# Constant matmuls into score banks, mask rows in another order, and a moved step table in an attention-to-experts kernel

## The chip, the cores and the metric

The kernel runs on one core of a Trainium2 chip. The metric is the device time of one execution in microseconds (us), as the median of several runs. A profile is one more execution, recorded by the hardware; its clock for an instruction's start counts from the first instruction. The engines are named as the profile names them: PE is TensorE (matmuls and transposes), PEld its weight loads, DVE is VectorE, ACT is ScalarE, POOL is GpSimd, SP is the engine that issues most DMAs.

## The reference

Clustered attention, then a routed layer of eight experts, then a dense layer.

```python
q_assign = np.argmax(np.einsum('bhsd,hcd->bhsc', q_n, c_n), axis=-1)   # 16 clusters
k_assign = np.argmax(np.einsum('bhsd,hcd->bhsc', k_n, c_n), axis=-1)
mask = q_assign[:, :, :, None] == k_assign[:, :, None, :]
scores = np.where(mask, scale * np.matmul(q, k.transpose(0, 1, 3, 2)), -1e9)
attn = softmax(scores); out = np.matmul(attn, v)       # B=2, H=8, S=768, D=64
...
e_idx = np.argmax(x @ w_gate, axis=1)                  # one of 8 experts for each of 1536 tokens
h = np.maximum(x[mask] @ w1[e], 0.0); ye = h @ w2[e]   # 512 -> 1024 -> 512
out[mask] = gate_w[mask, None] * eom[mask, e, None] * ye
...
h = x @ w_in; g = h * sigmoid(h); out = g @ w_out      # 512 -> 2048 -> 512
```

## The kernel before

**Attention** goes over eight pairs of heads (four in each of two batches), twelve steps a pair, 96 steps in all. A step is 128 queries of one head against all 768 keys. The scores of a step are four matmuls into a two-bank tile `sp` of which two copies exist (`qk_mm`, L398 and L400). The first two multiply `QA` by `KA`, which hold the split values; the second two multiply `QB` by `KB`, whose rows 64 to 79 hold a one-hot cluster number, so that a product of unequal clusters is pushed out of the softmax. DVE takes the minimum of the (negated) scores (`m`, L419), ACT the exponential (`p`, L421), which also frees `sp`. The weights of attention are then split in a high and a low 16-bit part and turned, in one of two ways. In the steps for which `onpe` holds (two of each six, and all of the last twelve), PE transposes them (`ptp`, L445), ACT writes the high part (`pt`, L451) and DVE subtracts to get the low one (`low2`, L456). In the others the high part is a copy by ACT (L430), or by DVE where `dve` says so (L464), POOL subtracts (L465), and a DMA transposes. `pv` then multiplies with the values (L489 to L491) into `o`, and DVE normalises `o` into `xb` (L496 to L498).

Between the steps stand the preparations of the next pair, at steps that a table of numbers gives (`plan`, `prepare`): loads, splits, transposes of q and k (`tp`, L190), products with the centroids (`cl`, L207), the search for the nearest one in four pieces (`best`, L217 to L225, which ends in the one-hot rows `oh`), and the mask rows (`masks`: transposes L365, one ACT operation to `mk`, four DMAs into `QB` and `KB`). The first pair has no step before it: `first` makes its heads, and `masks1` writes their mask rows straight from PSUM, three one-hot tiles at a time. `T` tiles (three PSUM banks) serve all transposes, centroid products, masks and logits.

**Order.** All attention instructions of an engine run in the order in which the code records them: `run` adds a dependency from each to the one before it on its engine. An engine waits at its next instruction, and what is behind waits too.

**The router.** When both heads of a pair are done, `Moe.pair` transposes their output (`xtp`, L717), multiplies by the router's weights (`lg`, L729) and adds to the logits (L736); after a batch's last pair `route` picks experts, ranks the tokens by matmuls (`rk`, L777 to L781) and scatters the rows to the experts' lists by indirect DMAs on POOL (L818). These are generators; `run` calls them so many times a step as a table of small numbers says. Step 84 starts the last pair; its queries are taken in two groups, four tiles then two, so that the last routing covers only two tiles.

**PE fillers.** `warm` issues matmuls of constant ones ahead of the first transposes, and 33 constant matmuls (L1075) stand between the last routing and the first expert. After that the experts (L1000, L1016) and the dense layer (L1246, L1225) run, fed by weights that SP loads and ACT, DVE and POOL split.

Of the kernel before, what the change touches and what calls it, by code (L numbers as in the profile page):

```python
# [30 lines left out]
class Att:  # L31
# [251 lines left out]
    def plan(s, pairs, g0, vg):  # L283

        nc = s.nc
        u = []
        add = lambda r, f: u.append((r, f))
        nx = lambda g: lambda: next(g, None)
        s.v1 = s.load_v(1)
        for r in (-0.5, 0.0, 0.0, 1, 1.5, 2, 3.0, 3.5):  # L290
            add(r, nx(g0))
        for r in (1.5, 1.5, 2.5, 3.5, 4.5, 5.5, 6, 6.5):
            add(r, nx(vg))
        for r in (13.5, 17.5, 23.0, 32.5, 33.5, 40.5, 41.5, 42.5, 44.0):
            add(r, nx(s.v1))
        for r in (-0.5, -0.5, 0.0, 0.5):
            add(r, lambda: s.bgdma.pop(0)())
        for p, (b, hp) in enumerate(pairs):
            o = 12 * p
            for h, r in enumerate((7.0, 10.0) if p == 0 else (1.5, 1.5)):  # L300
                add(o + r, lambda b=b, h=2 * hp + h: s.split_v(b, h))
            if p:
                s.prepare(add, p, pairs[p], o - 12)
        u.sort(key=lambda x: x[0])
        return u

    def prepare(s, add, p, pair, o):

        nc = s.nc
        b, hp = pair  # L310
        z = p == 1
        if not z:
            add(2.5 if p == 2 else o - 12 + -3.0, lambda: s.load_qk(b, hp))
        for i, r in enumerate((-1.0, -1.0) if z else (6.0, 9.5) if p == 2 else [o - 12 + r for r in (6.0, 6.0)]):
            add(r, lambda i=i: s.halves(pair, i))
        hd = [None, None]
        mem = {}
        ch = [None, None]

        def tr(j, a, half):  # L320
            if a == 0 and half == 0:
                hd[j] = s.heads(2 * hp + j, j)
            s.turned(hd[j][1 + 2 * a], s.nqk[pair][a], j, half, (-0.125, 1.0)[a])
            if half:
                src, dst, e = ((hd[j][1][0:64], hd[j][2][0:64], nc.sync), (hd[j][3][64:128], hd[j][4][0:64], nc.sync))[a]
# [11 lines left out]
        for x, r in zip(tr8, (1.5, 1.5, 2.0, 2.5, 3.0, 4.5, 5.5, 5.5) if z else (-1.5, -1.0, -1.0, -0.5, 0.5, 1.5, 3.5, 3.5)):  # L337
            add(o + r, lambda x=x: tr(*x))
        for (j, a), r in zip(((0, 0), (0, 1), (1, 0), (1, 1)), (4.0, 5.0, 6.0, 6.5) if z else (0.5, 1.0, 4.0, 4.0)):
            add(o + r, lambda j=j, a=a: sc(j, a))  # L340
        for i, r in enumerate((5.5, 6.0, 7.0, 7.0, 7.5, 8.5, 9.0, 9.0) if z else (2.5, 2.5, 3.5, 4.5, 5.0, 5.0, 6.0, 7.5)):
            add(o + r, lambda j=i // 4: next(ch[j]))

        def m():
            s.masks(mem['oh'], hd)
            for j in range(2):
                s.ready[b, hp, j] = hd[j]
        add(o + (9.5 if z else 8.0), m)
# [22 lines left out]
    def masks1(s, oh, hd, j):  # L371

        nc = s.nc
        tps = []
        for half in range(2):
            for a in range(2):
                mp = s.T('mp1')
                tps.append(mp)
                for i in range(3):
                    nc.tensor.matmul(mp[64:80, i * 128:(i + 1) * 128], lhsT=oh[:, half * 3 + i, j, a], rhs=s.identb, start=True, stop=True)  # L380
            for a, w in ((0, 2), (1, 4)):
                dst = hd[w][64:80, half * 3:half * 3 + 3]
                src = tps[2 * half + a][64:80, :384].rearrange('p (t n) -> p t n', t=3)
                if a == 0:
                    nc.scalar.activation(dst, src, AF.Copy, scale=-1.0, bias=1.0)
                else:
                    nc.vector.tensor_scalar(dst, src, BIG, None, op0=ALU.mult)
            yield

    def qk_mm(s, st):  # L390
        nc = s.nc
        h, QA, QB, KA, KB = st['hd']
        t = st['t']
        sp = s.ps_s.tile([128, 2, 512], F32, tag='S', name='sp')
        KAf = KA.rearrange('p t n -> p (t n)')
# [12 lines left out]

    def dve(s, st):

        return st['i'] % 12 in (2, 8, 10)

    def soft(s, st):
        nc = s.nc
# [88 lines left out]
    def run(s):  # L503
# [4 lines left out]
        nc = s.nc  # L508
# [15 lines left out]
        st = s.setup()  # L524
        s.consts()
        s.warm(12)
        next(st)
        next(g0)
        next(st)
        next(g0)  # L530
        s.late = []
        s.steps = steps = []
        s.cur = None
# [8 lines left out]
        n = len(steps)  # L542
        done = 0
        i = -1
        todo = []
        while done < n:
            s.now = i
            if i + 1 < n:
                st = steps[i + 1]
# [12 lines left out]
            late = 2 <= i < n + 2 and s.onpe(steps[i - 2])  # L562
            if late and (i - 1 >= n or s.onpe(steps[i - 1])):
                s.low2(steps[i - 2])
                late = False
            if 1 <= i < n + 1:
                (s.turn if s.onpe(steps[i - 1]) else s.low)(steps[i - 1])
            if late:
                s.low2(steps[i - 2])
                late = False  # L570
            while todo and todo[0][0] <= i:
                todo.pop(0)[1]()
            for k in range(3 if i >= n - 12 else 2):
# [12 lines left out]
            if i == 86:  # L586
# [1 line left out]
                    s.bgdma.pop(0)()  # L588
                rg.append(s.route0)
                free = True  # L590
            for k in range((1, 0, 1, 2, 2, 1, 0, 1, 1, 2, 1, 0)[i % 12] if i < n - 12 else (2, 1, 0, 1, 1, 1, 2, 1, 2, 1, 1, 2)[i % 12] if i < n - 2 else (3, 1, 1, 0, 4)[i - n + 2]):
                if rg and (free or not (1 <= i < n - 12 and s.onpe(steps[i - 1]))):
                    x = next(rg[0], 0)
                    free = x == 'free'
                    if x == 0:
                        rg.pop(0)
# [34 lines left out]
class Moe:  # L631
# [112 lines left out]
    def route(s, b, att, g):  # L744
        nc = s.nc
        n = len(g)
# [566 lines left out]
```

## Time and profile before

| | |
|---|---|
| median of 3 runs | 793.61 us (791.09 to 793.64) |
| profiled execution | 794.19 us, of which the span of instructions is 792.5 us |
| PE busy | 742.1 us of the span (94%), 5498 matmuls |
| DVE, ACT, POOL busy | 467.7, 433.7 and 318.1 us |
| mean granted PE clock | 0.97 of full speed |
| first scores, last scores | 15.01 us, 252.37 us |
| first expert's transposes | 278.38 us |

The profiled execution lies 0.6 us over the median. Busy times are sums over the whole span, and stages have different limits; the clock column of a stretch, in which 1.00 is 2.4 GHz and 0.50 is 1.2 GHz, says whether a busy PE is busy at full speed.

### The profile page before, as it was taken

What the parts mean: (1) busy time and instruction counts of PE and PEld (TensorE: products, weight loads), DVE (VectorE), ACT (ScalarE), POOL (GpSimd) and SP (SyncE); (2) the same over time, 40 slices, a digit from 0 to 9 for tenths busy, and PEclk for the clock granted to TensorE, in tenths of its full rate; (3) what the DMA queues carried; (4) which work ended last, traced back from release to release, by engine and by line L of the source; (5) the groups of instructions that cost most, each with busy time, mean ns of one, the idle gap of its engine ahead of it and who ended that gap; (6) DMA issues with size and microseconds to landing.
All of it is one profiled execution on the core that took longest, in us unless ns stands there. A gap on an engine that the chain in (4) does not pass through costs nothing.

```text
span 792.5 us, 14080 instructions
## 1 busy us (share of the span) xinstructions
PE 742.1 (94%) x5498; PEld 625.6 (79%) x5498; DVE 467.7 (59%) x830; ACT 433.7 (55%) x703; POOL 318.1 (40%) x259
## 2 busy tenths in 40 slices
PE   7889999999997799999999999799999999999996
PEld 6788998999887478888978877587687888878885
DVE  6769887977785565555557683789524222232222
ACT  5769889988764435654556663788423222122222
POOL 5677878788631365443334552445300000000000
PEclk8779999999988899999999999999999999999999
DMA  8879998998993377876658735756101000010001
GB/s 270 173 151 215 200 181 176 188 195 179 196 171 121 137 259 229 296 268 230 205 159 285 261 116 191 242 166 207 34 1 53 1 1 0 1 54 0 1 1 55
DMA packets 132983, 116.30 MB, mean 147 GB/s; under 512 B 97607, under 2 KB 103751, under 8 KB 132912
## 3 DMA queue, kind: packets, MB, share of 16 engines
q1 hardware_dynamic: 129632, 109.03, 52.0%
q0 software_dynamic: 3280, 6.33, 2.1%
q8 instruction: 44, 0.72, 0.4%
q14 instruction: 27, 0.22, 0.1%
HBM read 71.67 MB, written 18.45 MB: 114 GB/s over the span
## 4 chain that ended last, share of the span: by engine, by line
PE 53%; DVE 14%; issue 11%; DMA 10%; ACT 6%; POOL 5%; POOLq 0%; ACTq 0%; DVEq 0%; SPq 0%
PE op L1225 14%; PE hp L1246 13%; DMA stage<-in_moe_w 4%; PE yp L1016 4%; PE sp L398 3%; PE hp L1000 3%; POOL w L899 3%; PE sp L400 3%; DVE m L419 3%; DMA x<-ys,f 3%; DVE pt L456 2%; PE tp L190 2%; ACT p L421 2%; PE ptp L445 2%; DMA stage<-in_moe_w_out 2%
## 5 line engine op out<-in xcount | busy, mean ns | idle before, releaser
L899 POOL TENSOR_TENSOR w<-stage,w 128x512 fp32r<-128x512 f32 (+1 forms) x54 | 101.3, 1880 | 120.5 <-ACT w L894 113.8
L1246 PE MATMUL hp<-XH,w 128*128 128x512 f32 (+1 forms) x392 | 124.3, 394 | 3.9 <-DVE sg L1253 3.1
L894 ACT ACTIVATE w<-stage 128x1024 fp32r<-128x1024 f32 (+1 forms) x104 | 96.6, 942 | 55.0 <-DMA stage<-in_moe_w 30.2
L419 DVE TENSOR_REDUCE m<-sp 128x1 f32<-128x768 f32 x96 | 91.2, 952 | 38.8 <-PE sp L400 34.0
L1225 PE MATMUL op<-w,GH 128*128 128x512 f32 x384 | 113.2, 397 | 0.0
L465 POOL TENSOR_TENSOR p<-p,p 128x768 f16<-128x768 f32 x58 | 95.2, 1650 | 38.3 <-DVE p L464 27.8
L1253 DVE TENSOR_TENSOR sg<-hp,sg 128x512 f32<-128x512 f32 (+1 forms) x49 | 33.3, 679 | 118.2 <-ACT sg L1252 118.2
L421 ACT ACTIVATE p<-sp,m 128x768 f32<-128x768 f32 x96 | 86.3, 899 | 16.1 <-DVE m L419 15.4
L1000 PEld LDWEIGHTS hp<-X,w 128*128 128x128 f32 x672 | 86.1, 188 | 11.0 <-DVE HL L1002 5.8
L1000 PE MATMUL hp<-X,w 128*128 128x256 f32 x672 | 89.8, 283 | 4.0 <-DVE HL L1002 3.1
L1252 ACT ACTIVATE sg<-hp 128x512 f32<-128x512 f32 (+1 forms) x49 | 28.8, 589 | 116.8 <-PE hp L1246 115.8
L1246 PEld LDWEIGHTS hp<-XH,w 128*128 128x128 f32 x392 | 73.2, 188 | 23.0 <-DVE sg L1253 4.8
L1225 PEld LDWEIGHTS op<-w,GH 128*128 128x128 f32 x384 | 71.9, 188 | 17.5 <-ACT GH L894 0.7
L899 DVE TENSOR_TENSOR w<-stage,w 128x1024 fp32r<-128x1024 f32 x50 | 67.9, 1371 | 28.9 <-ACT w L894 27.3
L1246 PE MATMUL hp<-XL,w 128*128 128x512 f32 (+1 forms) x196 | 75.1, 391 | 1.6 <-DVE XL L899 1.6
L1225 PE MATMUL op<-w,GL 128*128 128x512 f32 x192 | 68.3, 397 | 1.3 <-DVE GL L899 1.3
L1016 PE MATMUL yp<-w,HH 128*128 128x512 f32 x224 | 63.7, 401 | 3.0 <-ACT HH L1001 2.7
L489 PE MATMUL o<-vh,pt 128*128 128x66 f16 x576 | 64.6, 198 | 0.4 <-DVE pt L456 0.4
L491 PE MATMUL o<-vh,pt 128*128 128x66 f16 x576 | 63.5, 195 | 1.5 <-issue 1.5
L398 PE MATMUL sp<-KA,QA 128*128 128x384 f32 x192 | 61.0, 400 | 3.2 <-ACT p L421 2.7
L490 PE MATMUL o<-vl,pt 128*128 128x64 f16 x576 | 63.9, 194 | 0.2 <-issue 0.2
L489 PEld LDWEIGHTS <-pt 128*128 128x128 f16 x576 | 53.6, 99 | 9.7 <-issue 8.6
(216 smaller groups left out, 1432.3 us busy)
## 6 DMA issues: line engine op xcount, KB each, us to landing
stage<-in_moe_w SPq DMA_DIRECT2D x72, 512.0 KB
stage<-in_moe_w_in SPq DMA_DIRECT2D x16, 512.0 KB
stage<-in_moe_w_out SPq DMA_DIRECT2D x16, 512.0 KB
xst<-z SPq DMA_DIRECT2D x8, 516.0 KB
xt<-xst SPq DMA_DIRECT2D x6, 516.0 KB
vt<-in_v SPq DMA_DIRECT2D x4, 768.0 KB
xt<-x SPq DMA_DIRECT2D x6, 512.0 KB
out_x<-os SPq DMA_DIRECT2D x12, 256.0 KB
```

What stands on the lines that cost most here:

```text
L398: nc.tensor.matmul(sp[:, g, :384], lhsT=QA[:, t], rhs=KAf[:, g * 384:(g + 1) * 384], start=True, stop=False)
L419: st['min'] = nc.vector.tensor_reduce(m, sv, axis=AX.XY, op=ALU.min).ins
L421: st['exp'] = nc.scalar.activation(p32, sv, AF.Exp, bias=m, scale=-1.0).ins
L465: s.nc.gpsimd.tensor_sub(p16[:, 1], p32, p16[:, 0])
L489: nc.tensor.matmul(o[:, t, 0:D + 2], lhsT=pt[:, 0, kt], rhs=vh[:, kt], start=kt == 0, stop=False)
L490: nc.tensor.matmul(o[:, t, 0:D], lhsT=pt[:, 0, kt], rhs=vl[:, kt], start=False, stop=False)
L894: s.nc.scalar.activation(hi, src, AF.Copy)
L899: f = lambda: (eng or s.nc.vector).tensor_sub(lo, src, hi).ins
L1000: nc.tensor.matmul(hp, lhsT=W1[k][w][:, f * 128:(f + 1) * 128], rhs=x[:, k, :N], start=n == 0, stop=n == 11)
L1016: nc.tensor.matmul(yp, lhsT=h[:, f, i * 128:(i + 1) * 128], rhs=w, start=n == 0, stop=n == 23)
L1225: nc.tensor.matmul(op[i], lhsT=g[:, i * 128:(i + 1) * 128], rhs=w, start=f == 0 and m == 0, stop=f == 15 and m == 2)
L1246: nc.tensor.matmul(h, lhsT=I[k, f // 8][w][:, fs], rhs=x[:, k, c], start=n == 0, stop=n == 11)
```

## The change

Constant matmuls of 512 columns are put ahead of the scores of the first 16 steps and of most of the last 16, into the score tile that the scores then overwrite; eleven more `warm` matmuls stand ahead of and behind the transpose of the centroids. `masks1` writes the key rows first, one half by DVE and one by ACT, and hands over after three of the four pieces and after the fourth (before: two and two). The copy of step 10 of each pair goes from DVE to ACT. A `low2` that stood ahead of `pv` now stands behind it. The first batch's six scatters are recorded two at a time. Most numbers of the step table move by half a step to a few steps, and those of the router's table change.

```diff
-        for i, r in enumerate((-1.0, -1.0) if z else (6.0, 9.5) if p == 2 else [o - 12 + r for r in (6.0, 6.0)]):
+        for i, r in enumerate((-1.0, -0.5) if z else (6.0, 8.0) if p == 2 else [o - 12 + r for r in (6.0, 6.0)]):
...
-        for i, r in enumerate((5.5, 6.0, 7.0, 7.0, 7.5, 8.5, 9.0, 9.0) if z else (2.5, 2.5, 3.5, 4.5, 5.0, 5.0, 6.0, 7.5)):
+        for i, r in enumerate((5.5, 6.0, 6.0, 7.5, 7.5, 8.0, 9.0, 9.0) if z else (2.5, 2.5, 4.0, 5.0, 5.0, 5.0, 6.5, 7.0)):
...
     def masks1(s, oh, hd, j):
-        for half in range(2):
-            for a in range(2):
-                mp = s.T('mp1')
-                for i in range(3):
-                    nc.tensor.matmul(mp[64:80, i * 128:(i + 1) * 128], lhsT=oh[:, half * 3 + i, j, a], rhs=s.identb, start=True, stop=True)
-            for a, w in ((0, 2), (1, 4)):
-                if a == 0:
-                    nc.scalar.activation(dst, src, AF.Copy, scale=-1.0, bias=1.0)
-                else:
-                    nc.vector.tensor_scalar(dst, src, BIG, None, op0=ALU.mult)
-            yield
+        put(0, 1, nc.vector)
+        put(1, 1, nc.scalar)
+        put(0, 0, nc.vector)
+        yield
+        put(1, 0, nc.scalar)
+        yield
...
         sp = s.ps_s.tile([128, 2, 512], F32, tag='S', name='sp')
+        for _ in range(s.idle.get(st['i'], 0)):
+            nc.tensor.matmul(sp[:, 0], lhsT=s.ones, rhs=s.ones.unsqueeze(1).to_broadcast([128, 4, 128]), start=True, stop=True)
...
-        return st['i'] % 12 in (2, 8, 10)
+        return st['i'] % 12 in (2, 8)
...
         next(g0)
+        s.warm(5)
         next(st)
+        s.warm(6)
         next(g0)
+        s.idle = dict(list(enumerate((1, 1, 1, 1, 1, 1, 1, 1, 1, 1, 1, 1, 1, 1, 1, 1))) + list(enumerate((0, 1, 2, 0, 1, 1, 1, 1, 1, 1, 1, 1, 1, 1, 1, 1), 80)))
...
                 (s.turn if s.onpe(steps[i - 1]) else s.low)(steps[i - 1])
-            if late:
-                s.low2(steps[i - 2])
-                late = False
...
-            for k in range((1, 0, 1, 2, 2, 1, 0, 1, 1, 2, 1, 0)[i % 12] if i < n - 12 else (2, 1, 0, 1, 1, 1, 2, 1, 2, 1, 1, 2)[i % 12] if i < n - 2 else (3, 1, 1, 0, 4)[i - n + 2]):
+            for k in range((2, 2, 1, 2, 1, 1, 2, 1, 0, 2, 1, 0)[i % 12] if i < n - 12 else (1, 1, 0, 1, 1, 1, 2, 1, 2, 1, 1, 2)[i % 12] if i < n - 2 else (2, 2, 1, 0, 2)[i - n + 2]):
...
-            if b or t == g[0]:
+            if b or (t - g[0]) % 2 == 0:
                 yield 'free'
             s.scatter(s.xst, s.slot[:, b * NT + t:b * NT + t + 1], xb[:, t], E * CAP)
```

PE, at the first three steps of the first pair, before (`sp` scores, `cl` centroid products of the second head):

```order
L398 MATMUL sp<-KA,QA 128x384 x2
L400 MATMUL sp<-KB,QB 128x384 x2
L207 MATMUL cl<-cQ,QA 128x32 x6
L207 MATMUL cl<-cK,KA 128x32 x6
L398 MATMUL sp<-KA,QA 128x384 x2
L400 MATMUL sp<-KB,QB 128x384 x2
```

The same place of the changed kernel, whose lines 402 and 404 are the former 398 and 400:

```order
L398 LDWEIGHTS ones
L398 MATMUL sp<-ones 128x512
L402 MATMUL sp<-KA,QA 128x384 x2
L404 MATMUL sp<-KB,QB 128x384 x2
L207 MATMUL cl<-cQ,QA 128x32 x6
L207 MATMUL cl<-cK,KA 128x32 x6
L398 LDWEIGHTS ones
L398 MATMUL sp<-ones 128x512
```

One constant matmul stands ahead of each step's scores, behind whatever the score tile waits for; nothing else moved here.

DVE, around step 9 of the first pair, before (`cl`, `mx` and `oh` are the last pieces of the search of the next pair's first head, `pt` the low part of step 7):

```order
L419 TENSOR_REDUCE m<-sp 128x1
L464 CAST p_624<-p_622 128x768
L456 TENSOR_TENSOR pt<-ptp,pt 128x384 x2
L222 TENSOR_TENSOR cl<-cl,rev 128x192
L223 TENSOR_REDUCE mx<-cl 128x12
L225 TENSOR_TENSOR oh<-cl,mx 128x2x6x16
```

The same place of the changed kernel (its L423, L468 and L460 are the former L419, L464 and L456):

```order
L423 TENSOR_REDUCE m<-sp 128x1
L468 CAST p_647<-p_645 128x768
L222 TENSOR_TENSOR cl<-cl,rev 128x192
L223 TENSOR_REDUCE mx<-cl 128x12
L225 TENSOR_TENSOR oh<-cl,mx 128x2x6x16
L460 TENSOR_TENSOR pt<-ptp,pt 128x384 x2
```

The two subtractions moved behind the one-hot rows.

DVE, in the last routing, before (`xb`, `rs` and `o` are the last two tiles' outputs and their normalisation, `slot` and `r_g` end the routing of the four tiles ahead of them):

```order
L804 TENSOR_TENSOR slot<-rank,r_sk 128x4
L805 SCALAR_TENSOR_TENSOR r_g<-r_ev,r_g 128x4
L806 RECIPROCAL xb_67<-r_g 128x4
L496 TENSOR_SCALAR rs<-o_4851,vsc_2346 128x2
L497 RECIPROCAL rs<-rs 128x2
L498 TENSOR_TENSOR xb_67<-o_4851,rs 128x2x64
```

The same operations in the changed kernel:

```order
L772 TENSOR_TENSOR moe_oh<-r_eq,r_mx 128x4x8
L500 TENSOR_SCALAR rs<-o_4895,vsc_2353 128x2
L501 RECIPROCAL rs<-rs 128x2
L502 TENSOR_TENSOR xb_67<-o_4895,rs 128x2x64
L787 TENSOR_TENSOR r_d_4939<-lacc_108,moe_oh 128x32
```

The normalisation moved ahead of the second half of the four tiles' routing (L787 to L810, formerly L783 to L806). On PE, in the same part of the program, the six `xtp` transposes and the twelve logit matmuls of pair 6 stood ahead of the scores of steps 94 and 95; now three transposes stand ahead of step 95's scores and the rest behind them. On POOL the six scatters of the first batch follow each other as before, with the same waits.

## Rows read from the trace of the kernel before

**Rows 1.** Busy us (instructions) of each engine, PE clock and DMA, by stretch

```profile
core 0: us, PE busy (x) PEld busy (x) DVE busy (x) ACT busy (x) POOL busy (x), PEclk, DMA share, GB/s
16.00:31.00 15.00, 12.34 (x77) 10.46 (x76) 13.55 (x23) 11.63 (x18) 10.07 (x7) 0.89 0.69 182
78.40:105.20 26.80, 26.65 (x364) 24.82 (x362) 24.10 (x46) 23.31 (x38) 21.70 (x19) 1.00 0.99 187
222.00:235.00 13.00, 12.68 (x176) 11.89 (x175) 12.40 (x34) 9.54 (x19) 1.09 (x2) 0.99 1.01 169
```

**Rows 2.** The same view: stretches of attention at half clock

```profile
31.20:41.40 10.20, 10.20 (x42) 9.59 (x42) 6.63 (x13) 6.66 (x12) 7.47 (x7) 0.50 1.00 190
44.80:51.60 6.80, 6.07 (x53) 5.60 (x54) 3.10 (x5) 3.53 (x6) 6.15 (x7) 0.50 0.21 44
215.50:222.30 6.80, 6.21 (x49) 5.51 (x50) 3.26 (x7) 1.80 (x2) 6.49 (x10) 0.50 0.95 210
242.80:249.60 6.80, 5.38 (x40) 4.82 (x40) 3.86 (x8) 3.30 (x7) 0.00 (x0) 0.50 0.11 41
```

**Rows 3.** The same view: what each engine did just before the clock fell

```profile
4.00:10.70 6.70, 3.54 (x27) 3.03 (x28) 4.36 (x23) 3.91 (x9) 2.68 (x3) 1.00 1.02 290
26.00:31.20 5.20, 3.74 (x26) 3.07 (x24) 4.33 (x9) 4.80 (x8) 3.55 (x3) 1.00 1.09 244
239.00:242.80 3.80, 2.29 (x21) 1.71 (x18) 0.21 (x1) 0.28 (x1) 2.92 (x3) 1.00 0.54 209
```

**Rows 4.** PE alone, line 1075 (constant matmuls of 512 columns), at half and full clock

```profile
268.10:273.40 5.30, 5.30 (x13) 1.90 (x14) 0.50 0.88 338
273.60:278.00 4.40, 4.40 (x21) 1.81 (x19) 1.00 0.44 135
```

**Rows 5.** Timeline of PE: start, length, what, [idle before it, and what ended that]

```profile
14.75 0.33 PE L380 MATMUL mp<-identb,oh 128*16 128x128 bf16 x3 [0.41 <-DVE KB L387]
45.53 0.85 PE L365 MATMUL mp<-identb,oh 128*64 128x128 bf16 x6 [2.57 <-DVE oh L225]
...
216.09 1.01 PE L400 MATMUL sp<-KB,QB 80*128 80x384 f32 x2 [1.26 <-DMA KB<-mk]
245.94 0.90 PE L717 MATMUL xtp<-ident,xb 128*128 128x128 f32 x3 [0.58 <-ACT xt L719]
251.04 1.49 PE L729 MATMUL lg<-wr,xt 128*128 128x16 f32 x12
256.08 0.52 PE L445 MATMUL ptp<-ident,p 128*128 128x128 f32 x3 [1.18 <-DVE pt L456]
```

**Rows 6.** Timeline of DVE in the first pair

```profile
35.00 0.18 DVE L154 COPY vsc<-vps 128x16 f32<-128x16 f32 x1 [1.04 <-PE vps L151]
37.74 0.57 DVE L217 TENSOR_REDUCE cl<-cl 128x192 f32<-128x384 f32 x1 [0.64 <-PE cl L207]
39.13 0.96 DVE L419 TENSOR_REDUCE m<-sp 128x1 f32<-128x768 f32 x1 [0.83 <-PE sp L400]
43.40 1.02 DVE L456 TENSOR_TENSOR pt<-ptp,pt 128x384 f16<-128x384 f32 x2
47.99 0.96 DVE L419 TENSOR_REDUCE m<-sp 128x1 f32<-128x768 f32 x1 [1.65 <-PE sp L400]
```

**Rows 7.** Timeline of DVE in the last routing

```profile
261.87 0.19 DVE L783 TENSOR_TENSOR r_d<-lacc,moe_oh 128x32 f32<-128x32 f32 x1
263.58 0.19 DVE L496 TENSOR_SCALAR rs<-o,vsc 128x2 f32<-128x2 f32 x1
```

**Rows 8.** The two kinds of copy, by line: ns least/median/most, first and last start

```profile
L464 DVE CAST p<-p x21: 549/552/722, 25.8 to 213.4; 128x768 f16<-128x768 f32 x21
L430 ACT ACTIVATE p<-p x37: 844/846/848, 18.1 to 214.5; 128x768 f16<-128x768 f32 x37
```

**Rows 9.** Timeline of POOL and PE where attention hands over to the experts

```profile
272.24 0.98 POOL L818 DMA_INDIRECT xst<-xb,slot  x1 [0.31 <-issue]
278.38 1.32 PE L956 MATMUL etp<-ident,xt 128*128 128x128 f32 x8 [0.34 <-DMA xt<-xst]
```

More of the change, by code (lines that the diff above doesn't have):

```diff
@@ L289, in plan @@
         s.v1 = s.load_v(1)
-        for r in (-0.5, 0.0, 0.0, 1, 1.5, 2, 3.0, 3.5):
+        for r in (-0.5, 0.0, 0.5, 1, 1.5, 2, 3.0, 3.5):
             add(r, nx(g0))
-        for r in (1.5, 1.5, 2.5, 3.5, 4.5, 5.5, 6, 6.5):
+        for r in (1.5, 1.5, 2.0, 4.0, 4.5, 5.5, 6, 6.5):
             add(r, nx(vg))
-        for r in (13.5, 17.5, 23.0, 32.5, 33.5, 40.5, 41.5, 42.5, 44.0):
+        for r in (14.0, 17.0, 23.5, 34.0, 34.0, 40.5, 41.5, 43.0, 43.5):
             add(r, nx(s.v1))
-        for r in (-0.5, -0.5, 0.0, 0.5):
+        for r in (-0.5, 0.5, 1.5, 1.5):
             add(r, lambda: s.bgdma.pop(0)())
@@ L299, in plan @@
             o = 12 * p
-            for h, r in enumerate((7.0, 10.0) if p == 0 else (1.5, 1.5)):
+            for h, r in enumerate((7.0, 11.0) if p == 0 else (0.5, 2.0)):
                 add(o + r, lambda b=b, h=2 * hp + h: s.split_v(b, h))
@@ L312, in prepare @@
         if not z:
-            add(2.5 if p == 2 else o - 12 + -3.0, lambda: s.load_qk(b, hp))
-        for i, r in enumerate((-1.0, -1.0) if z else (6.0, 9.5) if p == 2 else [o - 12 + r for r in (6.0, 6.0)]):
+            add(2.0 if p == 2 else o - 12 + -2.5, lambda: s.load_qk(b, hp))
+        for i, r in enumerate((-1.0, -0.5) if z else (6.0, 8.0) if p == 2 else [o - 12 + r for r in (6.0, 6.0)]):
             add(r, lambda i=i: s.halves(pair, i))
@@ L336, in prepare @@
         tr8 = [(j, a, half) for j in range(2) for a in range(2) for half in range(2)]
-        for x, r in zip(tr8, (1.5, 1.5, 2.0, 2.5, 3.0, 4.5, 5.5, 5.5) if z else (-1.5, -1.0, -1.0, -0.5, 0.5, 1.5, 3.5, 3.5)):
+        for x, r in zip(tr8, (1.5, 1.5, 2.0, 2.5, 3.0, 4.5, 5.5, 5.5) if z else (-1.5, -1.0, -0.5, 0.0, 0.5, 1.5, 3.5, 3.5)):
             add(o + r, lambda x=x: tr(*x))
-        for (j, a), r in zip(((0, 0), (0, 1), (1, 0), (1, 1)), (4.0, 5.0, 6.0, 6.5) if z else (0.5, 1.0, 4.0, 4.0)):
+        for (j, a), r in zip(((0, 0), (0, 1), (1, 0), (1, 1)), (4.5, 5.0, 6.5, 6.5) if z else (0.5, 1.0, 4.0, 4.0)):
             add(o + r, lambda j=j, a=a: sc(j, a))
-        for i, r in enumerate((5.5, 6.0, 7.0, 7.0, 7.5, 8.5, 9.0, 9.0) if z else (2.5, 2.5, 3.5, 4.5, 5.0, 5.0, 6.0, 7.5)):
+        for i, r in enumerate((5.5, 6.0, 6.0, 7.5, 7.5, 8.0, 9.0, 9.0) if z else (2.5, 2.5, 4.0, 5.0, 5.0, 5.0, 6.5, 7.0)):
             add(o + r, lambda j=i // 4: next(ch[j]))
@@ L373, in masks1, with put @@
         nc = s.nc
-        tps = []
-        for half in range(2):
-            for a in range(2):
-                mp = s.T('mp1')
-                tps.append(mp)
-                for i in range(3):
-                    nc.tensor.matmul(mp[64:80, i * 128:(i + 1) * 128], lhsT=oh[:, half * 3 + i, j, a], rhs=s.identb, start=True, stop=True)
-            for a, w in ((0, 2), (1, 4)):
-                dst = hd[w][64:80, half * 3:half * 3 + 3]
-                src = tps[2 * half + a][64:80, :384].rearrange('p (t n) -> p t n', t=3)
-                if a == 0:
-                    nc.scalar.activation(dst, src, AF.Copy, scale=-1.0, bias=1.0)
-                else:
-                    nc.vector.tensor_scalar(dst, src, BIG, None, op0=ALU.mult)
-            yield
+        def put(half, a, eng):
+            mp = s.T('mp1')
+            for i in range(3):
+                nc.tensor.matmul(mp[64:80, i * 128:(i + 1) * 128], lhsT=oh[:, half * 3 + i, j, a], rhs=s.identb, start=True, stop=True)
+            dst = hd[(2, 4)[a]][64:80, half * 3:half * 3 + 3]
+            src = mp[64:80, :384].rearrange('p (t n) -> p t n', t=3)
+            m, c = ((-1.0, 1.0), (BIG, 0.0))[a]
+            if eng is nc.scalar:
+                eng.activation(dst, src, AF.Copy, scale=m, bias=c)
+            else:
+                eng.tensor_scalar(dst, src, m, c, op0=ALU.mult, op1=ALU.add)
+        put(0, 1, nc.vector)
[4 more added lines that the diff above has]
+        yield
     def qk_mm(s, st):
```

## The prediction

> **What bounds the kernel now.** I first cut the span into stretches and read each engine's busy time and the granted clock together. In a pair of the middle PE is busy 26.65 of 26.80 us at full clock [rows 1], so attention's middle is PE's, and the experts behind it take whatever time attention ends earlier. Two parts of attention look otherwise. From 16 to 31 us DVE is busy 13.55 of 15.00 and PE 12.34: the first steps are DVE's. And four stretches run at 0.50, the lower of the clock's two levels (1.2 of 2.4 GHz): 31.2 to 41.4, 44.8 to 51.6, 215.5 to 222.3 and 242.8 to 249.6 us, with PE busy 10.20, 6.07, 6.21 and 5.38 [rows 2]. They lie in the first and the last pair, where the change puts its constants. The third view asks what PE did just before a fall: busy 3.74 of 5.20 and 2.29 of 3.80 us, with many short gaps; the fall at 10.7 follows 3.54 of 6.70 [rows 3]. Then come the timelines of PE and DVE with the wait ahead of each instruction, for what PE waits for where it is not busy [rows 5 to 7].
>
> **Price of a constant.** A matmul of 512 columns takes 4.40 / 21 = 0.21 us at full clock and 5.30 / 13 = 0.41 at half [rows 4]. In the same rows the clock rises while nothing but such constants runs. In the first row of [rows 2], on the other side, PE is busy at every moment and the clock stays down for the whole stretch. [...] The Trainium skill ("TensorE: Matmul & The Clock Gate", Part 1, "What's actually happening") says that the throttled state is the default and that a busy PE releases it. By that rule alone the constants could do nothing from 31.2 to 41.4 us, where PE is busy already; the row disagrees with it in this plain form, since a PE so busy should have been at full clock.
>
> **The change, part by part** (against the profiled execution's 794.19 us, span 792.5; minus is a gain).
>
> a) First mask rows. One-hot transposes at 14.75 us wait 0.41 for a copy of DVE [rows 5]. With the two halves' copies on DVE and ACT side by side and three of four pieces before the handover, this wait goes and a little of the copies' chain. I take -0.6, between 0 and -1.0 (the wait, the 0.33 behind it and a quarter for the copy).
>
> b) 31.2 to 41.4 us at full clock. PE's 10.20 busy us would halve to 5.10, which is the bound. But DVE works 6.63 and ACT 6.66 us in there, and DVE was the slower one just before, so they take over. What they idle for PE is 1.04 + 0.64 + 0.83 = 2.51 [rows 6]; most of that is what can be won. -2.0, between 0 and -5.1.
>
> c) One-hot rows ahead of two subtractions. The mask transposes of the second pair wait 2.57 us for `oh` [rows 5]; the subtractions moved behind `oh` take 1.02 [rows 6]. They are then late for step 7's `pv`, which has a step of slack. -1.0, between 0 and -1.0.
>
> d) 44.8 to 51.6: PE busy 6.07 at half clock; DVE has only 3.10 and ACT 3.53 in it, and DVE waits 1.65 for scores at 47.99 [rows 2, 6]. No other engine is near, so the half is won: -3.0, between 0 and -3.0.
>
> e) The 16 constants of the first pair and the step after it. Those of steps 0 to 11 fall where DVE sets the pace (PE idles 15.00 - 12.34 = 2.66 us from 16 to 31 alone [rows 1], more than 12 x 0.21) or into a stretch that gets shorter by b and d. The four of steps 12 to 15 lie where PE sets it: 4 x 0.21 = +0.9. Between 0 and 16 x 0.21 = +3.4.
>
> f) The 15 late constants. Four stand in steps 81 to 84, ahead of the 1.26 us for which PE waits on the mask rows' DMA [rows 5]: 0.84 is covered, and would cost that if the DMA were earlier. Eight (steps 85 to 92) stand where PE is busy 12.68 of 13.00 [rows 1]: 8 x 0.21 = +1.7. The last three stand in the gaps of [rows 3]. Between +0.6 (three uncovered) and 15 x 0.21 = +3.2.
>
> g) 215.5 to 222.3: PE busy 6.21, DVE 3.26, ACT 1.80 [rows 2]: half of it, -3.1, between 0 and -3.1. POOL's 6.49 are subtractions and copies that are taken up two steps later.
>
> h) 242.8 to 249.6: PE busy 5.38 would give -2.7. DVE and ACT have 3.86 and 3.30 there [rows 2], in a chain of output, transposes, copy (PE waits 0.58 for `xt` [rows 5]) that does not get faster. I take -1.5, between 0 and -2.7.
>
> i) The end of attention. The logits, 1.49 us as a block at 251.04 ahead of step 95's scores, and a wait of 0.58 leave that place [rows 5]. But PE waits 1.18 at 256.08 for a subtraction behind them, so part of the win is a longer wait there: -1.0 of the 2.07. On DVE the normalisation waits behind the four tiles' routing from 261.87 to 263.58, 1.71 us [rows 7]; it goes ahead of it, and the last two tiles' chain, which ends in the scatter at 272.24 and the first expert's transposes at 278.38 [rows 9], starts earlier. The four tiles' own scatters then come later and precede the last ones on POOL, so I take a third: -0.5. Together -1.5, between 0 and -3.8 (2.07 + 1.71).
>
> j) At nothing. The seven copies that go from DVE (0.552) to ACT (0.846) [rows 8]: ACT has 26.80 - 23.31 = 3.49 us free in a pair [rows 1], one copy takes 0.85 of them; without the cover 7 x 0.85 = +5.9. The eleven `warm` matmuls of half a constant's columns stand in PE's gaps before 10.7 us (3.16 of 6.70 us free [rows 3]); they would cost 11 x 0.1 = 1.1 without. The order of `low2` and `pv`, the table's numbers in the middle pairs: PE stays 99% busy and its work is the same. The scatters: POOL's rows do not move. The Trainium skill (same page, Part 4, "PE-mode transpose") says that transposes do not raise the clock as matmuls do; no run so far shows that by itself, and the sum does not use it.
>
> Sum: -0.6 - 2.0 - 1.0 - 3.0 + 0.9 + 1.7 - 3.1 - 1.5 - 1.5 = -10.1, so 784.1. The median of the three runs lies 0.6 below the profiled execution and the runs spread over 2.6, so I leave it at 784.1.
>
> **The rivals.**
>
> *Half of the clock.* The constants lift some of the four stretches and not others, or the fall comes later and shorter. For it: a step brings one constant, 0.21 us in some 2.2 (26.80 / 12), and PE idled 1.46 us in the 5.20 ahead of the second fall, so little is added. Terms b, d, g, h make -9.6; half of them gone gives 784.1 + 4.8 = 788.9.
>
> *The clock is not held at all.* Then -9.6 goes and constants in half-clock stretches cost 0.41. The stretches make 30.6 us; a step takes twice 2.23 there, so some seven constants, 2.9 us, of which three were charged 0.6: 784.1 + 9.6 + 2.3 = 796.0. For it: the stretch of 10.20 busy us at 0.50. Against: [rows 4], where the same matmul stands through the rise.
>
> *Slower: the constants lie on every step's chain.* A constant writes the score tile, so it starts only when the exponential has freed it, and the scores wait behind it. Where DVE and ACT set the pace this puts it on the path even though PE is idle on the average. If in addition the clock stays down, 31 x 0.41 = 12.7, less a, c and i (3.1): 794.19 + 9.6 = 803.8. It decides from the point where PE's gaps are waits for the tile and not for other data. Against: DVE's waits in the first pair are short, and two copies of the tile exist.
>
> *The scatters matter.* While they run, PE idles 3.80 - 2.29 = 1.51 us from 239 to 242.8 [rows 3] in spite of a DVE and an ACT that do almost nothing (0.21 and 0.28). If two at a time opens these gaps, another -1.5, and h in full, -1.2: 781.4. Against: POOL does the same work in the same order.
>
> **How the numbers follow.** The forecast 0.48, half of the clock 0.24, clock not held 0.14, slower 0.06, scatters 0.08. The range is 778 (the last case with a and i at their bounds, -0.4 and -2.3, rounded) to 795, which leaves out the slow case and most of the unheld clock, under 2 in 10. 0.5% is 4.0 us, about what a measurement of this kernel tells from no change: below 789.6 is faster. That holds for the forecast, the scatters and somewhat over half of the half case: 0.48 + 0.08 + 0.14 = 0.70; the rest of that case and most of the unheld clock are the same, 0.22; slower 0.08.
>
> **What the profile after would show.** For b, d, g and h: a granted clock near 1.00 from 16 to 55 us and around the last pair's start, and the first expert's transposes near 268 in place of 278. For c: a wait ahead of the mask transposes of about 1.5 in place of 2.57. For e and f: constants of 0.21 each, with no wait of DVE behind them. For i: the normalisation ahead of the routing and no lone block of logits ahead of step 95. For the copies: ACT below 25 of 26.8 in a middle pair. I am wrong if the clock still falls in the first pair, if DVE or ACT idle longer for scores while PE is at full clock, if middle pairs take other than 26.8 us, or if what attention wins is lost between the last scatter and the first expert.

## The result and the profile after

The changed kernel takes 786.05 us (median of 6 runs, 782.74 to 788.28) against 793.18 (6 runs, 791.09 to 794.25): ratio 0.9912, 95% interval 0.9886 to 0.9939. Measured again beside other kernels it was 785.83 against 795.07, ratio 0.9894 (0.9851 to 0.9937). The forecast was 784.1 out of 794.19, a ratio of 0.987: somewhat more was forecast than came, and the time lies inside the range. Its single terms are another matter, and most of this part is about them.

The first lines of the page after. Its execution took 786.47 us.

```profile
span 784.6 us, 14152 instructions
PE 739.1 (94%) x5540; PEld 624.2 (80%) x5540; DVE 462.6 (59%) x823; ACT 436.8 (56%) x710; POOL 316.2 (40%) x259
```

The stretches of [rows 1, 2] in the changed kernel, columns as there:

```profile
16.00:31.00 15.00, 12.24 (x75) 10.02 (x75) 12.94 (x21) 12.01 (x19) 9.47 (x6) 0.89 0.54 154
31.20:41.40 10.20, 10.09 (x71) 8.79 (x69) 8.61 (x22) 9.67 (x18) 7.81 (x8) 1.00 1.04 197
44.80:51.60 6.80, 3.74 (x53) 3.26 (x52) 1.69 (x3) 3.83 (x7) 6.65 (x8) 0.81 0.89 210
78.40:105.20 26.80, 26.66 (x364) 24.95 (x362) 22.66 (x44) 24.44 (x40) 22.10 (x19) 1.00 0.99 186
215.50:222.30 6.80, 6.65 (x87) 5.77 (x86) 4.09 (x9) 5.06 (x7) 5.76 (x6) 1.00 0.86 132
242.80:249.60 6.80, 6.08 (x109) 5.71 (x105) 5.29 (x10) 3.90 (x7) 0.00 (x0) 1.00 0.25 81
```

Three of the four stretches are at full clock now, and the first holds 71 matmuls where it held 42. The fourth, 44.8 to 51.6, is not a stretch of slow matmuls any more but one in which PE has nothing to do: 3.74 busy of 6.80. The timeline of PE (start, length, what, idle before it) says why:

```profile
25.51 1.51 PE L190 MATMUL tp<-ident,nk 128*128 128x128 f32 x6 [1.43 <-DVE KB L384]
43.31 0.52 PE L365 MATMUL mp<-identb,oh 128*64 128x128 bf16 x6 [1.87 <-DVE oh L225]
46.18 0.69 PE L402 MATMUL sp<-KA,QA 128*128 128x384 f32 x2
49.93 0.98 PE L404 MATMUL sp<-KB,QB 80*128 80x384 f32 x2 [3.06 <-DMA QB<-mk]
```

Step 12, the first of the second pair, has its first scores at 46.18 us, 4.1 us earlier than before, and then waits 3.06 us for its mask rows. The clock falls again at 49.1 us, near the end of this wait, and stays down to 55.9.

To see where the time went, I read the start of the same operation in each trace. Each number below is one start on PE (scores are L398 before, L402 after; the last column is the span); what lies between two columns is a stage.

| kernel | first scores | step 17 | step 80 | step 95 | first expert | dense layer | span |
|---|---|---|---|---|---|---|---|
| before | 15.01 | 63.37 | 204.93 | 252.37 | 278.38 | 502.91 | 792.5 |
| after | 16.51 | 65.36 | 206.67 | 247.48 | 273.55 | 494.02 | 784.6 |
| after, again | 15.41 | 62.05 | 203.45 | 244.25 | 270.25 | 492.37 | 782.7 |

From step 80 to step 95 it is 6.6 us less in both executions of the changed kernel (47.44 to 40.81 and to 40.80). The middle is as before (141.56, then 141.31 and 141.40). Up to step 17 one execution lost 1.99 and the other won 1.32. From the last score to the first expert nothing changed (26.01, 26.07, 26.00). The experts gave 4.06 and 2.41, though their own code is the same, so half of the 7.9 us between the first two spans is no term of the forecast.

### The profile page after: what moved, and what is told of

Its sections match the earlier page's. It is cut to its first block, busy times and chain, and to the rows that moved or that the text cites. A ratio compares the mean times of both kernels' runs of the same rounds, so it can differ in the third digit from the quotient of the medians.

```text
span 784.6 us, 14152 instructions
## 1 busy us (share of the span) xinstructions
PE 739.1 (94%) x5540; PEld 624.2 (80%) x5540; DVE 462.6 (59%) x823; ACT 436.8 (56%) x710; POOL 316.2 (40%) x259
## 5 line engine op out<-in xcount | busy, mean ns | idle before, releaser
L423 DVE TENSOR_REDUCE m<-sp 128x1 f32<-128x768 f32 x96 | 91.1, 950 | 42.4 <-PE sp L404 32.3
L402 PE MATMUL sp<-KA,QA 128*128 128x384 f32 x192 | 61.5, 401 | 2.2 <-ACT p L425 1.6
L493 PE MATMUL o<-vh,pt 128*128 128x66 f16 x576 | 63.1, 196 | 0.4 <-DVE pt L460 0.4
L495 PE MATMUL o<-vh,pt 128*128 128x66 f16 x576 | 62.2, 193 | 0.0
```

Of the source, the lines that this page charges most:

```text
L423: st['min'] = nc.vector.tensor_reduce(m, sv, axis=AX.XY, op=ALU.min).ins
L493: nc.tensor.matmul(o[:, t, 0:D + 2], lhsT=pt[:, 0, kt], rhs=vh[:, kt], start=kt == 0, stop=False)
L495: nc.tensor.matmul(o[:, t, 0:D + 2], lhsT=pt[:, 1, kt], rhs=vh[:, kt], start=False, stop=kt == NT - 1)
```

## The experiments

Twelve kernels ran in three sets of four, each beside the kernel before. A median is over twelve runs, over six for the changed kernel itself. Ratios are to the kernel before in the same set; its medians were 795.07, 791.87 and 793.36 us. A profile is one execution of each kernel.

**The changed kernel again.** No edit.

> The changed kernel once more, for a second profile. In its first profile the last pair gained 7 us against the kernel before, the first pair lost 2, the experts gained 4. If these belong to the kernel, the new profile shows the same three numbers within 1 us; if they depend on the execution (where the clock's records begin, how loads meet), the first pair and the experts differ by 2 us or more. Time 784 to 788.

It took 785.83. The last pair's gain came out the same to 0.01 us; the first pair differed by 3.3 us and the experts by 1.7. So what one profile shows of the first pair, and part of what it shows of the experts, belongs to an execution. Here PE waits 2.83 us for `oh`, and not for the mask rows:

```profile
44.49 0.52 PE L365 MATMUL mp<-identb,oh 128*64 128x128 bf16 x6 [2.83 <-DVE oh L225]
```

**Constants, by leaving them out of the changed kernel or adding them to the one before.** One line is edited, here with its three new forms: none, late ones only, early ones only (the kernel before gets the loop in `qk_mm` too):

```diff
-        s.idle = dict(list(enumerate((1, 1, 1, 1, 1, 1, 1, 1, 1, 1, 1, 1, 1, 1, 1, 1))) + list(enumerate((0, 1, 2, 0, 1, 1, 1, 1, 1, 1, 1, 1, 1, 1, 1, 1), 80)))
+        s.idle = {}
+        s.idle = dict(list(enumerate((0, 1, 2, 0, 1, 1, 1, 1, 1, 1, 1, 1, 1, 1, 1, 1), 80)))
+        s.idle = dict(list(enumerate((1, 1, 1, 1, 1, 1, 1, 1, 1, 1, 1, 1, 1, 1, 1, 1))))
```

None, in the changed kernel:

> The changed kernel without its 31 constants ahead of scores. Theory (the constants hold the clock in the last pair): the clock falls to half in the last pair again, attention there is 4 to 6 us longer, 789 to 792 us in all. Rival (the gain comes from the tables and the order at the end): 31 constants less work, 783 to 786 us.

Late ones only, in the changed kernel:

> The changed kernel with the 15 late constants only. Theory (the first pair's constants win nothing, since PE waits 3.06 us for the mask rows' DMA at step 12 and the clock falls there all the same): 784 to 787, like the changed kernel. Rival (they hold the clock from 31 to 41 us, and DVE and ACT would not give the time back): 788 to 791, with the clock at half in the first pair for some 14 us.

Early ones only, in the changed kernel:

> The changed kernel with the 16 early constants only. Theory (the late ones hold the clock): half clock in the last pair, 789 to 792. Rival (the order holds it): 784 to 786.

Late ones only, in the kernel before:

> The kernel before with the 15 late constants and nothing else. Theory (the constants alone hold the clock in the last pair): no half clock from 210 to 250 us, 788 to 790.5 us. Rival (they need the tables): the clock falls somewhere in the last pair, 793 to 796.

All 31, in the kernel before:

> The kernel before with all 31 constants and nothing else. Theory (in the first pair they hold the clock, and the time comes back in the wait for the mask rows): first pair 0 to 2 us shorter, in all 787 to 790. Rival (the whole gain is the constants'): 785 to 787, the changed kernel's time.

| constants | in the changed kernel | in the kernel before |
|---|---|---|
| none | 790.53, ratio 0.9953 (0.9919 to 0.9987) | 1 |
| late | 789.94, 0.9928 (0.9890 to 0.9966) | 792.48, 0.9997 (0.9964 to 1.0030) |
| early | 787.96, 0.9956 (0.9928 to 0.9984) | not tried |
| all | 785.83, 0.9894 (0.9851 to 0.9937) | 788.57, 0.9934 (0.9905 to 0.9963) |

Of the five expectations the theory's time came with none in the changed kernel (but not its fall of the clock in the last pair, as shown below) and with all in the one before; with the late ones alone the changed kernel came out as the rival had it; the other two lie between the ranges. By the times, all 31 constants are worth 4.7 us in the changed kernel (790.53 to 785.83, same set, twelve runs against six, and the two ratios' intervals still overlap a little) and 3.3 in the one before, where the interval is clear of 1. Everything else in the change together is worth about half a per cent (0.9953). Neither half of the constants alone differs clearly from none.

Every timed run also has its mean granted clock on record, and it goes with the constants. In the kernel before it was 0.963 to 0.986 without them (the set in which all 31 were tried) and 0.983 to 0.991 with all 31. In the changed kernel it was 0.971 to 0.986 without (median 0.980) and 0.982 to 0.989 with all (twelve runs of the two sets; median 0.985). There, the four runs without constants that took less than 787 us had 0.984 to 0.986, and the seven that took more than 790 had 0.971 to 0.980. The late ones alone gave 0.979 in the changed kernel and 0.976 in the one before (medians; without them 0.980 and 0.975), the early ones alone 0.983.

The traces say something that I had not expected: the late ones are not needed for the clock in the last pair. Here are 200 to 256 us of the kernel before and then of the changed kernel without any constant:

```profile
200.00:256.00 56.00, 48.64 (x624) 43.87 (x622) 39.68 (x88) 34.11 (x57) 22.84 (x22) 0.88 0.76 166
```

```profile
200.00:256.00 56.00, 48.14 (x711) 42.96 (x707) 42.17 (x105) 35.16 (x63) 21.45 (x21) 1.00 0.70 162
```

Full clock throughout, with no constant. Steps 80 to 95 take 40.83 us there and 40.54 with the early ones alone, as with all (40.81). In the kernel before, the late ones alone bring steps 80 to 95 from 47.44 to 43.38 and keep the clock up:

```profile
200.00:256.00 56.00, 49.65 (x697) 44.76 (x696) 42.59 (x95) 36.94 (x62) 24.69 (x23) 1.00 0.76 172
```

So each of the two, new tables or constants, kept the clock up there in the execution that was profiled, and the tables take 2.6 us more off. The gain of the late ones in that profile does not show in the twelve timed runs of that kernel (ratio 0.9997), and with all 31 its clock fell once in the last pair (242 to 245.5 us; steps 80 to 95 take 43.89).

In the first pair the early ones raise the clock, without holding it. From 12 to 65 us its mean was 0.71 in the kernel before with late ones only, and 0.97 with all:

```profile
12.00:65.00 53.00, 49.03 (x385) 44.24 (x386) 38.41 (x70) 37.21 (x61) 36.67 (x33) 0.71 0.77 178
```

```profile
12.00:65.00 53.00, 45.67 (x432) 39.76 (x432) 41.99 (x76) 39.91 (x65) 39.38 (x34) 0.97 0.83 201
```

The time to step 17 went from 65.37 to 62.82 with it, 2.55 us for a clock that rose by a third (3.89 us counted from the first scores, which came 1.34 us later). Over all fourteen traces, from 18 to 65 us, the mean clock is 0.89 to 0.96 in the eight with early constants and 0.74 to 0.89 in the six without. The time does not follow as closely: the changed kernel with no constant goes from first scores to step 17 in 44.80 us, with all in 48.85 and 46.64. A warning comes with the kernel without constants: its profiled execution took 785.78 us, the second fastest of its twelve (785.67 to 796.27). Its longer runs have a lower clock; where in the program it falls, no profile shows.

**Eleven `warm` matmuls out of the changed kernel.**

```diff
         next(g0)
-        s.warm(5)
         next(st)
-        s.warm(6)
```

> The changed kernel without the eleven constants of 256 columns around the transpose of the centroids. In its profile they ran at half clock (0.21 and 0.18 us each) between 8.2 and 10.6 us and the first scores came 1.5 us later than before. If they are on the path, the first scores come 1 to 2 us earlier and the time is 784 to 785.5; if they bring the clock up for what follows, no change or up to 1 us slower.

786.54, ratio 0.9919 (0.9890 to 0.9949): no difference from the changed kernel that these intervals can tell, and first scores at 16.56, where the profiles with them had 16.51 and 15.41. So the first case of the expectation, that they are on the path and cost 1 to 2 us, did not come. The traces show a price and a gain. The same six transposes take 0.85 us at the start of the profile before and 1.51 or 1.52 in the other thirteen, which is the pace of half clock (1.51 at 11.81 us before, where the column reads 0.50), though the clock column reads 1.00 there. Before, then the changed kernel, with its clock:

```profile
5.60 0.85 PE L190 MATMUL tp<-ident,nq 128*128 128x128 f32 x6 [1.76 <-DVE nq L241]
```

```profile
5.58 1.52 PE L190 MATMUL tp<-ident,nq 128*128 128x128 f32 x6 [1.75 <-DVE nq L241]
4.00:10.70 6.70, 5.12 (x25) 4.39 (x25) 4.33 (x21) 4.21 (x9) 1.57 (x2) 1.00 1.02 292
```

In all ten traces with the `warm` matmuls the pace is full from 11.7 us on at the latest, by the centroid products (0.82 us for six, 1.44 at the slow pace). Without them it stays slow to 16 us and more in two of the three traces that start slow (first scores at 16.56 and 16.86). The eleven take about the time that they give back.

**The fourth pair's loads behind the mask rows.** SP issues two loads of 384 KB just ahead of the four mask-row DMAs. Its timeline in the changed kernel:

```profile
42.41 0.58 SPq L181 DMA_DIRECT2D qld<-in_q  x1
43.04 0.45 SPq L181 DMA_DIRECT2D kld<-in_k  x1
44.88 0.59 SPq L369 DMA_DIRECT2D QB<-mk  x1
```

```diff
-            add(2.0 if p == 2 else o - 12 + -2.5, lambda: s.load_qk(b, hp))
+            add(2.0 if p == 2 else 11.5 if p == 3 else o - 12 + -2.5, lambda: s.load_qk(b, hp))
```

> The changed kernel with the two loads of the fourth pair (768 KB) two steps later, so that they stand behind the four mask-row DMAs on SP and not ahead of them. Theory (the mask rows wait in the queue behind these loads): PE's wait of 3.06 us ahead of step 12's second scores falls below 1, the clock does not fall there, 782 to 784.5 us. Rival (the mask rows' DMA has this latency by itself, or the transposes hold it): the wait stays above 2 us, 785 to 787.

The wait was gone: step 12 had its first scores at 47.37 and the second ones at 48.23, and step 17 came at 60.81, the second earliest of all fourteen traces. The clock still fell, from 44.5 to 48 us. And the kernel was slower than the changed one, against the expectation: 792.02, ratio 0.9965 (0.9938 to 0.9993). DVE paid for it, at the next pair's loads of `v`:

```profile
66.94 0.95 DVE L135 TENSOR_REDUCE vam<-vt 128x2 f32<-128x768 f32 x1 [4.19 <-DMA vt<-in_v]
```

DVE runs in its order, so the minimum of step 18 stood behind this wait, and PE, whose step 20 needs the score tile that step 18's exponential frees, waited 5.05 us for that. The clock fell behind it:

```profile
71.33 1.01 PE L402 MATMUL sp<-KA,QA 128*128 128x384 f32 x2 [5.05 <-ACT p L425]
68.50:75.50 7.00, 4.17 (x30) 4.02 (x31) 6.42 (x14) 4.86 (x7) 3.42 (x2) 0.51 1.11 215
```

Steps 17 to 23 hold all of the loss: 5.2 us more than in the changed kernel without constants, and no more behind them up to step 80. Before, SP issues this load 3.2 us ahead of step 17's scores (60.16 and 63.37); here it issues it at 60.88, with the scores at 60.81, and it lands about 6.1 us later, 4.8 to 4.9 in the four traces in which DVE waits less than 1 us for it. The same with the loads directly behind the mask rows (10.0 in the place of 11.5), with all constants and with the early ones only:

> The changed kernel with the fourth pair's two loads directly behind the four mask-row DMAs on SP (the later place let a load of v start late, for which DVE then waited 4.19 us). Theory: no wait for QB<-mk at step 12, steps 0 to 17 take 44.5 to 46.5 us, steps 17 to 80 stay at 141.5, and the time is 0.5 to 2 us below the changed kernel's. Rival: the later loads make the v load late here too, steps 17 to 80 above 143 and the time 787 or more.

> The same with the late 15 constants out. Theory (with the new tables the last pair holds the clock without them): steps 80 to 95 take 40.5 to 41.5 us, no half clock from 200 to 256, time as in the run with them, within 1.5 us. Rival (they matter in executions whose clock records lie otherwise): 3 us or more slower, as the timed runs of the kernel with the early ones alone suggested (788.0 against 785.8).

788.86, ratio 0.9944 (0.9909 to 0.9979), and 790.33, 0.9966 (0.9930 to 1.0002). Steps 0 to 17 take 45.90 and 43.90 us, steps 17 to 80 147.78 and 147.65: the rival of the first expectation. The wait for the mask rows is smaller but not gone, 0.82 and 0.80 us. Two rows with all constants:

```profile
48.88 0.59 PE L404 MATMUL sp<-KB,QB 80*128 80x384 f32 x2 [0.82 <-DMA QB<-mk]
68.01 0.95 DVE L135 TENSOR_REDUCE vam<-vt 128x2 f32<-128x768 f32 x1 [4.44 <-DMA vt<-in_v]
```

With the early ones only, steps 80 to 95 take 41.56 and the clock falls once in them (219.5 to 223 us), which the theory had excluded; so the new tables do not hold the clock there in every execution.

**One table back, without constants.** The router's step table and scatters of before:

```diff
-            for k in range((2, 2, 1, 2, 1, 1, 2, 1, 0, 2, 1, 0)[i % 12] if i < n - 12 else (1, 1, 0, 1, 1, 1, 2, 1, 2, 1, 1, 2)[i % 12] if i < n - 2 else (2, 2, 1, 0, 2)[i - n + 2]):
+            for k in range((1, 0, 1, 2, 2, 1, 0, 1, 1, 2, 1, 0)[i % 12] if i < n - 12 else (2, 1, 0, 1, 1, 1, 2, 1, 2, 1, 1, 2)[i % 12] if i < n - 2 else (3, 1, 1, 0, 4)[i - n + 2]):
...
-            if b or (t - g[0]) % 2 == 0:
+            if b or t == g[0]:
```

> The changed kernel without constants ahead of scores, and with the router's step table and scatters of before. Theory (the router's table shortens the last pair): steps 80 to 95 take 44 to 48 us and the clock falls there, 793 to 797 us. Rival (the preparations' table does it): 40.5 to 42 us, 789 to 791.

And, on its own, the numbers of `plan` and `prepare` of before:

> The changed kernel without constants ahead of scores, and with the preparations' step table of before (plan and prepare). Theory (the router's table shortens the last pair): steps 80 to 95 take 40.5 to 43 us with at most one short fall of the clock. Rival (the preparations' table does it): 45 to 48 us, the wait for KB<-mk at step 84 back at 1.26 us. Time 790 to 794.

792.57, ratio 1.0018 (0.9992 to 1.0044), and 794.80, 1.0043 (1.0005 to 1.0080), where both new tables give 0.9953. The first lies between its expectation's ranges, near the theory's; of the second the stage came as its theory has it, and the time lies 0.8 us above. Steps 80 to 95 take 43.62 and 41.86, each with one short fall of the clock, against 40.83. So, in one execution of each, the router's table with its scatters gives 2.8 us there and the preparations' 1.0; neither alone accounts for the 6.6. The old preparations cost 4.8 us elsewhere: steps 17 to 80 take 146.76 in place of 141.92. That they do not go with the edits that stayed, the copies on ACT and the `low2` behind `pv`, is a guess (not tried apart). PE's own waits from 80 to 200 us are small there (`tp` for `pt` 1.4 us in four, `tp` for `lacc` 0.8 in five, and few more), where the changed kernel has 0.8 in all.

## Why the prediction came out, term by term

**a, the start: -0.6 failed.** The wait of 0.41 is one of 0.31, and first scores stand at 16.51 and 15.41 after, 15.01 before. Over all traces they lie between 15.01 and 16.86, and they follow how early PE's pace rises from half (see the `warm` matmuls above) more than any edit of a. In the changed kernel's profile the added `warm` matmuls stand here, on the way to the centroids' transpose:

```profile
8.17 1.27 PE L69 MATMUL warm<-ones 128*128 128x256 bf16 x5
9.24 0.42 PE L96 MATMUL ctp<-ident,cd 128*128 128x128 f32 x1
```

Five in 9.24 - 8.17 = 1.07 us are 0.21 each, for 256 columns the pace of half clock by [rows 4], where the profile before had the same stretch at full clock: its transposes take 0.85 us where these take 1.52. The price of `warm` without cover, which j put at 1.1, shows in this execution. The runs without them were no faster, since in two of the three the products behind then run at the slow pace.

**b, c and d, the first pair: -6.0 failed in size.** The step that failed is "no other engine is near, so the half is won" (d), and with it the taking of b as paid out. The clock did come up from 31.2 to 41.4, and step 12's first scores come 4.10 us earlier. But it fell elsewhere ahead of step 17, for 10 and 7 us in the two executions, and a fall in the first pair was one of the prediction's own signs of being wrong. And step 12's second scores stand at 49.93 and, in the second execution, at 49.47 us, because behind each wait taken away stood the next. I had followed PE, DVE and ACT there, and not the queue that feeds them. The mask rows come through SP, 1.84 us behind a load of 384 KB in the changed kernel, 4.2 in its second execution and 5.9 before; with 1.84 they are 3.06 late. With the loads put behind, the wait went in one kernel and fell to 0.8 in the two others, which settles that one; then the load of `v` was late. c did not do what it should either: the wait of 2.57 became 1.87 and 2.83 us. I had named `pv` as what the later subtractions might delay, and took the whole 1.02.

The Trainium skill ("DMA: Bandwidth & Descriptors", "Two DMAs through the same engine are not ordered") says that within one queue of one DMA engine descriptors start in order. The traces go with it: in the four kernels with these loads ahead in which PE waits for the mask rows, PE goes on 5.05 us after the issue of the first 48 KB where that issue is 1.84 us behind the load's, 4.12 where it is 2.15 behind, and 2.9 where it is 3.7 behind. With the loads put behind it is still 2.8 us, so only what is above that is the load's.

**e, the 16 early constants: the price is not measured by itself.** Up to step 17 the kernel before wins 2.55 us net by them, in one execution of each; the changed kernel, in its profiles, wins nothing there.

**f, the late constants' price: +1.7 was too much.** From step 85 to step 92 seven constants are passed. Without them these steps take 229.83 - 215.16 = 14.67 us, with them 233.22 - 218.30 = 14.92: 0.25 in place of 7 x 0.21 = 1.5. The other traces at full clock there agree: 14.91 to 14.93 in five more of the changed order with the late constants, 14.67 and 14.69 in two more without. The row that I read, PE busy 12.68 of 13.00, I took for PE setting the pace; DVE's 12.40 of 13.00 stood beside it. (It begins at 222 us, and two of the eight steps, 85 and 86, start ahead of it, at 217.91 and 220.35.) The same 13 us of these steps, in the kernel without constants and then with them:

```profile
218.00:231.00 13.00, 12.68 (x177) 11.78 (x175) 12.65 (x35) 9.79 (x20) 3.89 (x7) 1.00 0.99 190
```

```profile
221.00:234.00 13.00, 13.00 (x182) 12.32 (x181) 12.60 (x35) 10.10 (x20) 4.27 (x8) 1.00 0.96 210
```

PE goes from 12.68 to all of it, and DVE keeps its 12.6: the constants fill what PE had free.

**g, h and the logits of i: -5.6 came as -6.6, for a reason that I had only in part.** The clock was the term, and it stays up in the last pair. But the constants are not what it takes: in two profiles without the late ones it stays up as well. The order was enough for it there; in three more profiles without them, each with one edit more, it fell once for some 3.4 us, and in the six of the changed order with them it never did. Two places changed. The wait for `KB<-mk` of 1.26 us at step 84 [rows 5] is filled with the constants ahead of it (it is 1.05 without any, with the same time from step 80 to 95, so this is not where the time comes from), and the logits are no block ahead of step 95's scores: steps 93 to 95 start at 238.92, 242.99 and 247.48, 8.56 us where it was 12.33. The twelve logit matmuls stand behind them now:

```profile
247.48 0.70 PE L402 MATMUL sp<-KA,QA 128*128 128x384 f32 x2
...
250.68 1.51 PE L733 MATMUL lg<-wr,xt 128*128 128x16 f32 x12 [0.58 <-ACT xt L723]
```

The rival that the scatters open PE's gaps by themselves has no row for it: PE is busy 4.76 of 7.80 us from 235.0 to 242.8, 4.69 before. The scatters were put back only together with the router's table, so they are not tried by themselves.

**i, the normalisation: -0.5 failed.** It moved as the order says, from behind the four tiles' routing to ahead of its second half. But the last score and the first expert lie as far apart as ever (26.01, 26.07). The scatters of POOL are why. Its timeline before (the first of four tiles' scatters, then the first of the last two tiles'):

```profile
263.95 1.00 POOL L818 DMA_INDIRECT xst<-xb,slot  x1 [1.08 <-DVE rs L496]
...
270.95 0.99 POOL L818 DMA_INDIRECT xst<-xb,slot  x1 [1.91 <-DVE o_cnt L840]
```

After, the first and last of the four, then the last two:

```profile
260.87 1.00 POOL L822 DMA_INDIRECT xst<-xb,slot  x1 [1.07 <-DVE lacc L740]
...
264.74 0.97 POOL L822 DMA_INDIRECT xst<-xb,slot  x1 [0.30 <-issue]
...
266.64 0.99 POOL L822 DMA_INDIRECT xst<-xb,slot  x1 [0.67 <-issue]
267.94 0.97 POOL L822 DMA_INDIRECT xst<-xb,slot  x1 [0.30 <-issue]
```

They follow each other with next to no gap, and the wait of 1.91 us ahead of the last two is gone. But the first of the four starts 13.39 us behind step 95's scores, 11.58 before, and the last of all 20.46, 19.87 before [rows 9]: what the last tiles' chain won stands behind the four scatters that came later. I had said so and still taken a third.

**j and the middle: right but for `warm` (see a).** Steps 17 to 80 are at 141.31 (141.56), ACT has 24.44 of 26.80 us in a middle pair, and PE 26.66.

**Not forecast: the experts.** They gave 4.06 and 2.41 us in the changed kernel. Over the other kernels, in which they are the same instructions, they take 220.6 to 226.1 us, and the 224.53 of the profile before lies inside that, so these gains can be the executions' alone.

As a whole: the first expert starts at 273.55 and 270.25 us, where I had said near 268. That the sum was near is luck in good part, because terms failed on both sides: the first pair's 6.6 (a to d) hardly came, f's 1.7 were not charged, and the last pair gave 1.0 more than its terms. (The lower end of the range is 781.4 - 0.4 - 2.3 = 778.7, rounded the wrong way; nothing hangs on it.)

Why are constants that the last pair does not need in a profile worth 4.7 us in the medians? The times are 782.7 to 788.3 with all (12 runs) and 785.7 to 796.3 with none (12 runs), and the recorded clocks say that the longer of the latter are those with a lower clock: 0.976 in the longest, 0.986 in the profiled one. Since a stretch at half clock takes half of its length off the mean, these two numbers and the span of 784 us give an estimate of 2 x 0.010 x 784 = 16 us more at half clock in the longest. With all constants no run had less than 0.982. So the constants take away executions in which the clock falls more. Where it falls in them stays open, since none of the longer executions was profiled; the medians of the recorded clock point to the early constants more than to the late ones. The order of `masks1`, the copies on ACT and the place of `low2` were in every changed kernel and were not taken back one by one. No version here is clearly faster than the changed kernel.

## What to carry to other kernels

Where a chain of waits is shortened at one end, follow the data back through the queue that carries it as well as through the engines: the mask rows, then the load of `v`, each became the floor of the next gain. An engine that is 97% busy beside another at 95% did not yet set the pace here, and filling it cost 0.25 us of the 1.5 that a sum of its work says. Constants for the clock are best judged by the medians, the spread and the mean clock of many runs, since one profile can be one of the fast executions. A reordering that closes PE's gaps did much of the same without them in one stage.

## What the runs showed of the hardware

The granted clock of one kernel differs between executions. In two executions of the changed kernel, the same instructions ran at half clock from 25.2 to 28.6 and 49.1 to 55.9 us in the one, and from 35.7 to 39.1 and 46.0 to 49.4 in the other, and first scores lay 1.1 us apart. At the very start the clock column can read 1.00 where the lengths of the same instructions say half (1.52 us against 0.85 for six transposes at 5.6 us). The kernel without score constants spread over 785.67 to 796.27 us in 12 runs. The Trainium skill ("TensorE: Matmul & The Clock Gate", "What's actually happening") says that the number of slow matmuls at the start varies from run to run, and puts the penalty of that start below 1% of a typical span; the first scores agree with the first part (1.85 us between extremes, 0.2% of the span), while the spread of that kernel, 1.3%, is more than the start's alone, and goes with the mean clock of the whole run (0.986 to 0.971).
